# An S4 convolution and mixer block on one core: the inverse transform of the first half moved to the last steps and the pause behind them, three store buffers, other queues for x and w1, w1 and w2 split later

## The chip, the cores and the metric

The kernel runs on one core of a Trainium2 chip. The metric is the device time of one execution in microseconds, as the median of several runs. All data are float32; on TensorE weights of the mixer are held as two float32r parts, a high and a low one.

## What is computed

With h a layer norm of x scaled and shifted by a conditioning vector, a state-space convolution over 2048 positions and 512 channels is added to x, then a token-mixing and a channel-mixing MLP. The reference, cut to what matters:

```python
def _A_ref(u, A_re, A_im, B_re, B_im, C_re, C_im, log_dt, Dskip):
    P = jnp.exp(logdA[:, :, None] * l[None, None, :])
    K = jnp.einsum("dn,dnl,dn->dl", Cc, P, dB).real
    Yf = rfft2(pad(up)) * rfft2(pad(K))
    return irfft2(Yf)[..., :L] + u * Dskip
def _B_ref(x, w1, w2, w3, w4):
    h = _gelu(_layernorm(x) @ w1)
    x1 = x + shifted_channel_groups(h) @ w2
    return x1 + _gelu(_layernorm(x1) @ w3) @ w4
x = A_u
h = _layernorm(x) * (1 + ca) + sa
x = x + ga * _A_ref(h, ...)
h = _layernorm(x) * (1 + cb) + sb
x = x + gb * _B_ref(h, w1, w2, w3, w4)
```

## The kernel before, in words

The order of every engine's instructions is the order in which the code records them; the tile framework adds the semaphore waits. SP, ACT and POOL issue DMAs, each in its own order, so a DMA that waits holds up what its engine issues after it. Stages:

1. *To about 212 us.* The convolution's kernel K is built (exponentials, sines, products on DVE, matmuls); x's first transform is written to DRAM as VU. On the side POOL copies w3, w4 and w2 to DRAM scratch (WD, L506 to L512).
2. *k_first (L619), 212 to 224.* Eight rounds of matmuls turn K (in KX) into the two halves VK[0], VK[1]. T2 and TU are tables; T3 holds negated columns of T2, made by POOL in `flip` (L658).
3. *The sixteen steps (L1096 to L1150), 225 to 304.* A step is (jh, kc): half jh of the channels, block kc of the frequencies. In step n PE does `spectrum_k` (sk, L680, 32 matmuls on T2, T3 and VK), then `back` of step n-1 (L702, with the table Gm), then `spectrum_u` of step n+1 (su, L650, on a VU block). DVE's `multiply` (L690, L692) makes four products and two sums, zc. ACT copies su's banks to us (three copies) and back's banks pz to z (two copies), and z is stored to DRAM as ZT[jh] by two DMAs of 256 KB on POOL. `load_vu` reads the VU block of a later step into a ring of seven blocks (ldp, tile "ld").
4. *Back over positions.* `inverse(jh, g)` (two `inv_half`, L726 to L734) takes four blocks of ZT[jh], reread by `load_inv` (L717), and the table FI, and adds the result to X2, the residual x, which `load_x` puts in the place of KX once k_first has read that. Groups g = 0 and 3 use blocks 0, 3, 4, 7; groups 1 and 2 use 1, 2, 5, 6. For the first half the four groups run in steps 12, 13, 15 and behind the steps, into the pz, pk2 and py banks of PSUM. `half_stat` (L783) takes half statistics of X2 rows.
5. *The hole (L1151 to L1181).* After the last step ZT[1] must be stored and reread before anything else can go on: about 304 to 316. PE runs dummy matmuls there (`keep`).
6. *The mixer.* Token mixing (w1, w2), then channel mixing (w3, w4); TensorE is nearly full there.

w1 and w2 are split by `weights` (L743): a load, then for each of four row blocks a copy to float32r on ACT (high part) and a subtraction on DVE (low part). Before, w1 is staged through the ldp ring and split in steps 9 and 10, w2 in steps 14 and 15. A z tile has two buffers, so the copy of step n waits for the store of step n-2.

Of the kernel before, what the change touches and what calls it, by code (L numbers as in the profile page):

```python
# [106 lines left out]
def body(ctx, tc, A):  # L107
# [439 lines left out]
    with tc.manual_schedule():  # L547
# [49 lines left out]
        for f in later:  # L597
# [6 lines left out]
    v0x = ExitStack()  # L604
    c2 = a2.enter_context(pool("c2"))
    TU = TU[0]
    Gm = c2.tile([128, 2, 64], F32, name="Gm")
    FI = c2.tile([128, 32, 2, 32], F32, name="FI")
    VK = [v0x.enter_context(pool("v0", side="right")).tile([128, 64, 2, 64], F32, name="VK0"),
          c2.tile([128, 64, 2, 64], F32, name="VK1")]  # L610
    ldp = a2.enter_context(pool("ldp", bufs=7))
    s2x = ExitStack()
    s2 = s2x.enter_context(pool("s2", bufs=2))
    psa = s2x.enter_context(pool("psa", bufs=2, space=PSUM))
# [38 lines left out]
            act(us[:, n], q[n % 2])  # L653
        return us

    t3s = {}

    def flip(kc):  # L658
        t = t3s[kc] = c2.tile([128, 8, 64], F32, name="T3", bufs=3)
        for gh in range(2):  # L660
            r = slice(gh * 64, gh * 64 + 64)
            P.tensor_scalar(t[r], T2[kc // 4][r, kc % 4 * 4:kc % 4 * 4 + 8, 64 - gh * 64:128 - gh * 64], -1.0, None, op0=OP.mult)

    def spectrum_k(jh, kc):
        p = [kbank([128, 2, 2, 128]) for gh in range(2)]
        for i in range(2):
            for ro in range(2):
                for ri in range(2):
                    for kk in range(2):
                        for gh in range(2):  # L670
                            k1 = kc * 4 + 2 * kk + i
                            rows = slice(gh * 64, gh * 64 + 64)
                            w = T2[k1 // 16][rows, k1 % 16]
                            if ri == gh:
                                w = w[:, ro * 64:ro * 64 + 64]
                            elif ro == ri:
                                w = w[:, gh * 64:gh * 64 + 64]
                            else:
                                w = t3s[kc // 2 * 2][rows, k1 % 8]
                            T.matmul(p[gh][kk * 64:kk * 64 + 64, i, ro], w,  # L680
                                     VK[jh][rows, ri * 32 + k1].rearrange("p j g -> p (j g)"),
                                     start=(ri == 0), stop=(ri == 1), skip_group_check=True)
        return p
# [10 lines left out]

    def back(jh, kc):
        zc = zcs.pop((jh, kc))
        z = s2.tile([128, 4, 256], F32, name="z")
        o = [psa.tile([128, 2, 256], F32, name="pz") for kk in range(2)]
        for n in range(2):
            for kk in range(2):  # L700
                r = slice(kk * 64, kk * 64 + 64)
                T.matmul(o[kk][n * 64:n * 64 + 64], Gm[r, n], zc[n][r], start=True, stop=True, skip_group_check=True)  # L702

        def store(q, a, b):
            for n in range(2):
                q.dma_start(dram(ZT[jh], n * 16384 + (kc * 4 + a) * 256, [[32768, 32], [8192, 2], [1, (b - a) * 256]]),
                            z[n * 64:n * 64 + 64, a:b].rearrange("p k d -> p (k d)"))

        last = (jh, kc) == (1, 7)
        for kk in range(2):  # L710
            act(z[:, 2 * kk:2 * kk + 2], o[kk])
            if last:
                store((Y, S)[kk], 2 * kk, 2 * kk + 2)
        if not last:
            store(P, 0, 4)

    def load_inv(jh, k, i=None, q=Y):  # L717
        if (jh, k) not in zis:
            zis[jh, k] = block()
        a, n = (0, 4) if i is None else (2 * i, 2)  # L720
        q.dma_start(zis[jh, k][:, a:a + n], dram(ZT[jh], (k * 4 + a) * 32768, [[256, 128], [32768, n], [1, 256]]))

    def load_x(g):
        Y.dma_start(X2[:, g * 4:g * 4 + 4].rearrange("p b d -> p (b d)"), A["x"][g])

    def inv_half(jh, g, i, pl, name):  # L726
        p = pl.tile([128, 2, 256], F32, name=name)
# [8 lines left out]
    def inverse_parts(jh, g, pl, name):  # L736
        return [inv_half(jh, g, i, pl, name) for i in range(2)]
# [5 lines left out]
    def weights(pl, src, rows, cols, name, ntile):  # L743
        hi = pl.tile([128, ntile, cols], F32R, name=name + "h")
        lo = pl.tile([128, ntile, cols], F32R, name=name + "l")

        def load(stage, i, m=1, c0=0, c1=cols):
            n = min(128, rows - i * 128)
            w = stage(m, c1 - c0) if stage else lo.bitcast(F32)[:, i:i + m, c0:c1]
            Y.dma_start(w[:n], src[i * 128:i * 128 + (m - 1) * 128 + n, c0:c1].rearrange("(a p) n -> p a n", p=n))  # L750

            def split():
                for j in range(m):
                    h = hi[:n, i + j, c0:c1]
                    act(h, w[:n, j])
                    V.tensor_sub(lo[:n, i + j, c0:c1], w[:n, j], h.bitcast(F32))  # L756
            return split
        return hi, lo, load

    def two(m, n):  # L760
        return block().rearrange("p (a c) b -> p a (c b)", a=2)

    def rstd(r, v):
        n = r.shape[-1]
# [326 lines left out]

    def split_w(n):
        for _ in range(n):
            splits.pop(0)()

    steps = [(jh, kc) for jh in range(2) for kc in range(8)]  # L1096
    with tc.manual_schedule():
        load_vu(*steps[0])
        flip(0)
        Y.dma_start(Gm, A["G"].rearrange("p (a b) -> p a b", a=2))  # L1100
        for r in range(8):
            k_first(r)
            if r == 3:
                load_vu(*steps[1])
            if r == 6:
                load_vu(*steps[2])
        us = spectrum_u(*steps[0])
        split = None
        for n, st in enumerate(steps):
            p = spectrum_k(*st)  # L1110
            multiply(*st, us, p)
            if n == 7:
                v0x.close()
                pw2 = ctx.enter_context(pool("pw2", side="right", reuse_waits="tile"))
                pw1 = ctx.enter_context(pool("pw1", side="right", reuse_waits="tile"))
                W2h, W2l, ldw2 = weights(pw2, WD["w2"], 512, 512, "w2", 4)
                W1h, W1l, ldw1 = weights(pw1, A["w1"], 512, 512, "w1", 4)
# [12 lines left out]
            if n == 9:  # L1130
                Y.dma_start(FI, A["FI"].rearrange("p (a b c) -> p a b c", a=32, b=2))
            if split:
                split()
                split = None
            if n in (8, 9):
                split = ldw1(two, n % 2 * 2, 2)
            if n == 10:
                for k in (0, 3, 4, 7):
                    load_inv(0, k)
            if n == 12:  # L1140
                inverse(0, 0)
                w2s = [ldw2(None, 2 * i, 2) for i in range(2)]
                for b in range(4):
                    half_stat(b, 0)
            if n == 13:
                inverse(0, 3)
                for k in (1, 2, 5, 6):
                    load_inv(0, k)
            if n in (14, 15):
                w2s.pop()()  # L1150
        for f in i1:  # L1151
            f()
        back(*steps[15])
        s2x.close()
        tp = lambda name, bufs=1, **k: pool(name, bufs, reuse_waits="tile", **k)
        cm = ctx.enter_context(tp("cm", 2, side="right"))
        hv = ctx.enter_context(tp("hv", side="right"))
        gop = ctx.enter_context(tp("gop", 2, side="right"))
        psT = ctx.enter_context(tp("psT", space=PSUM))
        psw = ctx.enter_context(tp("psw", 2, space=PSUM))  # L1160
        psy = a2.enter_context(tp("psy", 2, space=PSUM, side="right"))
# [4 lines left out]

        for k, i in ((3, 1), (0, 0)):
            load_inv(1, k, i, Y)
            load_inv(1, k + 4, i, S)
        for k, i in ((3, 0), (0, 1)):  # L1170
            load_inv(1, k, i)
            load_inv(1, k + 4, i)
        for i in range(2):
            inv_half(0, 2, i, psy, "py")()
        for b in (14, 15, 4, 5, 6, 7):
            half_stat(b, 0)
        for k in (1, 2):
            load_inv(1, k)
            load_inv(1, k + 4)
# [122 lines left out]
```

## Time and profile before

| | |
|---|---|
| runs, us | 688.12, 691.77, 688.82 (median 688.82) |
| profiled execution, us | 691.26 |
| its span, first to last instruction, us | 689.5 |
| mean granted TensorE clock | 0.989 |
| busy in the span: PE, DVE, ACT, POOL, us | 642.6, 498.0, 331.2, 124.8 |
| DMA over the span | 86.42 MB, mean 125 GB/s |

The span is the profiled execution's; 1.8 us lie around it. Times in the text are us from the start of the span. An instruction row gives start, length, engine, line, operation, out<-in with the shapes, a count, and in brackets the idle time before it with what ended it. A line may be that of a helper (L115 is every ACT copy), so the tile names tell what an instruction is: pz<-zc is back, pk<-ld su, pk<-VK sk, ZT<-z a store, ld<-VU and ld<-ZT the reads.

### The profile page before, as it was taken

The page shows a single profiled execution, that of the slowest core. Times are in us where ns is not written, and L with a number is a line of the kernel's source. Part 1 is how long each engine was busy: PE and PEld are TensorE (multiplying, and loading weights), DVE is VectorE, ACT ScalarE, POOL GpSimd, SP SyncE. Part 2 cuts the span into 40 slices and gives each one's busy share as a digit, 9 for nine tenths or more (in the row PEclk, how much of TensorE's full clock was granted, in tenths as well). Part 3 has the DMA queues.
Part 4 walks back from the last instruction along what each step waited for, and adds up shares of the span by engine and source line. Part 5 has one row for each costly group of instructions (what it writes and reads, how often), then busy time and mean ns, then how long its engine had stood idle before and what let it go on. Part 6 is the DMA issues. An engine that isn't in the chain of part 4 may idle for free.

```text
span 689.5 us, 16884 instructions
## 1 busy us (share of the span) xinstructions
PE 642.6 (93%) x7195; PEld 509.2 (74%) x7195; DVE 498.0 (72%) x795; ACT 331.2 (48%) x505; POOL 124.8 (18%) x236
## 2 busy tenths in 40 slices
PE   1899999999999998977998999999999999999996
PEld 0456655655569776634887889999899889898895
DVE  7899999999996887986987967464574536363522
ACT  3878988889875557432444623123131312222121
POOL 4011112112103355413741101001010000000000
PEclk9999999999999999998999999999999999999999
DMA  8603264643739997967387010020100201010001
GB/s 299 284 2 79 75 218 105 209 121 85 275 85 317 354 335 258 346 204 226 108 257 240 1 32 32 16 77 15 47 31 17 77 1 62 1 49 13 1 31 31
DMA packets 51091, 86.42 MB, mean 125 GB/s; under 512 B 4676, under 2 KB 39496, under 8 KB 48424
## 3 DMA queue, kind: packets, MB, share of 16 engines
q1 hardware_dynamic: 46712, 66.74, 30.1%
q0 software_dynamic: 3440, 17.57, 7.4%
q8 instruction: 56, 0.92, 0.6%
q10 hardware_dynamic: 864, 1.05, 0.5%
q14 instruction: 19, 0.16, 0.1%
HBM read 59.12 MB, written 32.90 MB: 133 GB/s over the span
## 4 chain that ended last, share of the span: by engine, by line
PE 70%; DVE 6%; DMA 5%; ACT 3%; POOL 2%; issue 1%; ACTq 0%; SPq 0%; DVEq 0%; POOLq 0%
PE pm L841 7%; PE pm L838 7%; PE pm L839 7%; PE xx L448 7%; PE pa L954 6%; PE pa L955 6%; PE pa L962 6%; PE kp L498 3%; DMA ZT<-z 3%; PE ph L893 2%; PE ph L895 2%; PE ph L892 2%; DMA ld<-ZT 2%; PE pu L426 2%; PE pT L803 2%; PE pk L626 2%
## 5 line engine op out<-in xcount | busy, mean ns | idle before, releaser
L115 ACT ACTIVATE gh<-pm 128x512 fp32r<-128x512 f32 (+1 forms) x48 | 26.9, 560 | 200.7 <-PE pm L841 200.7
L838 PE MATMUL pm<-nh,w3h 128*128 128x256 f32 (+1 forms) x352 | 86.6, 281 | 2.7 <-ACT nh L115 2.7
L839 PE MATMUL pm<-nh,w3l 128*128 128x256 f32 (+1 forms) x352 | 86.3, 280 | 0.1
L946 DVE TENSOR_TENSOR gl<-gf,gh 128x512 fp32r<-128x512 f32 (+1 forms) x48 | 30.8, 643 | 68.4 <-ACT gf L115 68.4
L954 PE MATMUL pa<-w4h,gh 128*128 128x512 f32 (+1 forms) x176 | 69.6, 395 | 0.0
L838 PEld LDWEIGHTS pm<-nh,w3h 128*128 128x128 f32 (+1 forms) x352 | 66.0, 187 | 4.4 <-ACT nh L115 2.9
L955 PE MATMUL pa<-w4l,gh 128*128 128x512 f32 (+1 forms) x176 | 68.9, 392 | 0.0
L839 PEld LDWEIGHTS pm<-nh,w3l 128*128 128x128 f32 (+1 forms) x352 | 65.9, 187 | 2.2 <-DVE w3l L756 0.5
L765 POOL TENSOR_TENSOR rs<-mv,eps_t 128x1 f32<-128x1 f32 (+1 forms) x39 | 11.0, 282 | 282.4 <-DVE mv L771 265.4
L841 PE MATMUL pm<-nl,w3h 128*128 128x256 f32 (+1 forms) x352 | 55.0, 278 | 0.0
L449 PE MATMUL xx<-MG,ON 64*128 64x512 f32 x160 | 48.1, 397 | 0.0
L962 PE MATMUL pa<-w4h,gl 128*128 128x512 f32 (+1 forms) x176 | 48.0, 390 | 0.0
L448 PE MATMUL xx<-MG,ON 64*128 64x512 f32 x160 | 48.0, 396 | 0.0
L841 PEld LDWEIGHTS pm<-nl,w3h 128*128 128x128 f32 (+1 forms) x352 | 47.0, 187 | 0.0
L898 DVE TENSOR_TENSOR h<-h,ph 128x512 f32<-128x512 f32 x16 | 11.0, 687 | 45.1 <-PE ph L895 45.1
L466 DVE SCALAR_TENSOR_TENSOR e<-tr,p 128x512 f32<-128x512 f32 x64 | 41.1, 684 | 1.5 <-ACT tr L115 1.5
L498 PEld LDWEIGHTS kp<-e,e 128*32 128x32 f32 x2048 | 30.1, 110 | 12.7 <-issue 7.6
L475 DVE TENSOR_TENSOR e<-tr,p 128x1024 f32<-128x1024 f32 x32 | 39.0, 1220 | 0.0
L476 DVE TENSOR_TENSOR e<-tr,m 128x1024 f32<-128x1024 f32 x32 | 39.0, 1219 | 0.0
L115 ACT ACTIVATE p<-xx 128x1024 f32<-128x1024 f32 (+1 forms) x40 | 37.5, 979 | 2.2 <-PE xx L252 1.0
L962 PEld LDWEIGHTS pa<-w4h,gl 128*128 128x128 f32 (+1 forms) x176 | 33.0, 188 | 7.3 <-DVE gl L946 0.2
L115 ACT ACTIVATE tr<-xx 128x1024 f32<-128x1024 f32 x32 | 33.0, 1030 | 9.6 <-PE xx L449 7.9
(236 smaller groups left out, 1731.6 us busy)
## 6 DMA issues: line engine op xcount, KB each, us to landing
VU<-vs SPq DMA_DIRECT2D x64, 128.0 KB, 3.7
ld<-VU SPq DMA_DIRECT2D x16, 512.0 KB, 7.4
ZT<-z POOLq DMA_DIRECT2D x30, 256.0 KB, 6.2
ld<-ZT SPq DMA_DIRECT2D x12, 512.0 KB
Dw<-in_w POOLq DMA_DIRECT2D x8, 688.0 KB, 4.7
xu<-in_u SPq DMA_DIRECT2D x4, 1024.0 KB, 8.0
KX<-in_x SPq DMA_DIRECT2D x4, 1024.0 KB, 8.0
GD<-go SPq DMA_DIRECT2D x16, 256.0 KB, 2.3
```

Of the source, the lines that this page charges most:

```text
L115: return S.activation(out, in_, f, bias=bias, scale=scale)
L448: T.matmul(x[:, :512], la, ma, start=(i == 0), stop=(i == len(ops) - 1))
L449: T.matmul(x[:, 512:], lb, mb, start=(i == 0), stop=(i == len(ops) - 1))
L466: V.scalar_tensor_tensor(e0[:, 1, a], tr[:, 1, 0], 1.0 - 2.0 * a, mg[:, a], op0=OP.mult, op1=OP.mult)
L475: V.tensor_mul(e0[:, 0], tr[:, 0, 0:1].to_broadcast([128, 2, 512]), mg)
L498: T.matmul(kp[32 * j:32 * j + 32, (k % 2) * 4 + g], e1[:, r, d], e0[:, r, :, d * 32:d * 32 + 32], start=(r == 0), stop=(r == 1), skip_grou ...
L838: T.matmul(p, wh[:, k, c], hi[k], start=(k == 0), stop=False)
L839: T.matmul(p, wl[:, k, c], hi[k], start=False, stop=False)
L841: T.matmul(p, wh[:, k, c], lo[k], start=False, stop=(k == 3))
L954: T.matmul(acc[i], gh[:m, e, s], W4h[:m, f], start=(f == 0), stop=False)
L955: T.matmul(acc[i], gh[:m, e, s], W4l[:m, f], start=False, stop=False)
L962: T.matmul(acc[i], gl[:m, e, s], W4h[:m, f], start=False, stop=(f == 10))
```

## The change

- z gets three buffers. T3 becomes one tile for all 32 frequencies, filled by eight POOL instructions before the steps; before, two instructions every second step filled one of three small tiles.
- The ldp ring has six blocks, not seven. Blocks 0, 3, 4, 7 of ZT[0] get four own buffers (zi), where VK[0] lay, and are read in step 9. w2's tiles, which lay there, come behind the steps.
- inverse(0, 0) moves from step 12 to step 14, inverse(0, 3) from 13 to 15, in the pz banks; group 1 moves behind back(15), its adds into the hole.
- x blocks and w1 are loaded by POOL's queue, w1 from a DRAM copy. FI is loaded before the steps. Gm takes FK's place, so its load follows k_first. A VU block is asked for four steps ahead, not three.
- w1: the high parts are copied in steps 13 and 14, the low parts made in the hole. w2 is loaded by POOL after the last steps and split wholly in the hole. Two rereads of ZT[1] go from ACT's queue to POOL's.

The diff, without its unchanged surroundings:

```diff
-    WD = {k: dpool.tile(list(A[k].shape), F32, name="D" + k) for k in ("w2", "w3", "w4")}
+    WD = {k: dpool.tile(list(A[k].shape), F32, name="D" + k) for k in ("w1", "w2", "w3", "w4")}
...
-        side[28 + 3 * k].append(lambda i=k * 256: P.dma_start(WD["w2"][i:i + 256], A["w2"][i:i + 256]))
+        for j, w in enumerate(("w1", "w2")):
+            side[24 + 4 * j + 2 * k].append(lambda w=w, i=k * 256: P.dma_start(WD[w][i:i + 256], A[w][i:i + 256]))
...
-    ldp = a2.enter_context(pool("ldp", bufs=7))
+    ldp = a2.enter_context(pool("ldp", bufs=6))
...
+    T3 = s2.tile([128, 32, 64], F32, name="T3", bufs=1)
+
+    def flip(i):
+        for a in range(0, 16, 8):
+            for gh in range(2):
+                r = slice(gh * 64, gh * 64 + 64)
+                P.tensor_scalar(T3[r, i * 16 + a:i * 16 + a + 8], T2[i][r, a:a + 8, 64 - gh * 64:128 - gh * 64], -1.0, None, op0=OP.mult)
...
-        z = s2.tile([128, 4, 256], F32, name="z")
+        z = s2.tile([128, 4, 256], F32, name="z", bufs=3)
...
-            zis[jh, k] = block()
+            zis[jh, k] = block() if jh or k in (1, 2, 5, 6) else zip_.tile([128, 4, 256], F32, name="zi")
...
-        Y.dma_start(X2[:, g * 4:g * 4 + 4].rearrange("p b d -> p (b d)"), A["x"][g])
+        P.dma_start(X2[:, g * 4:g * 4 + 4].rearrange("p b d -> p (b d)"), A["x"][g])
...
             if n > 0:
                 back(*steps[n - 1])
-            if n == 15:
-                i1 = inverse_parts(0, 1, psb, "pk2")
             if n < 15:
                 us = spectrum_u(*steps[n + 1])
-            if n + 3 < 16:
-                load_vu(*steps[n + 3])
-            if n % 2 == 0 and n < 14:
-                flip(steps[n + 2][1])
-            if n in (3, 4, 6, 8):
-                load_x(n - 3 if n < 5 else n // 2 - 1)
+            if n + 4 < 16:
+                load_vu(*steps[n + 4])
+            if n in (2, 4, 6, 8):
+                load_x((0, 3, 1, 2)[n // 2 - 1])
+            if n in (9, 10):
+                w1s.append(ldw1(None, n % 9 * 2, 2, q=P))
+            if n in (13, 14):
+                w1s[n - 13] = w1s[n - 13]()
             if n == 9:
-                Y.dma_start(FI, A["FI"].rearrange("p (a b c) -> p a b c", a=32, b=2))
...
-            if n == 10:
                 for k in (0, 3, 4, 7):
                     load_inv(0, k)
             if n == 12:
+                for k in (1, 2, 5, 6):
+                    load_inv(0, k)
+            if n == 14:
                 inverse(0, 0)
-                w2s = [ldw2(None, 2 * i, 2) for i in range(2)]
                 for b in range(4):
                     half_stat(b, 0)
-            if n == 13:
+            if n == 15:
                 inverse(0, 3)
...
         back(*steps[15])
+        i1 = inverse_parts(0, 1, psb, "pk2")
...
+        w2s = ldw2(None, 0, 4, q=P)
...
-            load_inv(1, k + 4, i, S)
+            load_inv(1, k + 4, i, P)
...
+        w2s = w2s()
+        for f in i1:
+            f()
         for i in range(2):
             inv_half(0, 2, i, psy, "py")()
         for b in (14, 15, 4, 5, 6, 7):
             half_stat(b, 0)
+        for f in w1s:
+            f()
+        w2s()
```

What this does to three queues. SP in the second part of the steps, before (ld<-VU a VU block, KX<-in_x an x block, ld<-in_w w1, ld<-ZT the rereads):

```order
L724 DMA KX<-in_x 128x2048
L750 DMA ld<-in_w 128x2x512
L640 DMA ld<-VU 128x4x256
L1131 DMA FI<-in_FI 128x2048
L750 DMA ld<-in_w 128x2x512
L640 DMA ld<-VU 128x4x256
L721 DMA ld<-ZT_61 128x4x256 x4
L640 DMA ld<-VU 128x4x256 x2
L750 DMA w2l<-Dw_64 128x2x512 x2
L721 DMA ld<-ZT_61 128x4x256 x4
```

and SP from its first VU block to the same place, after (FK<-in_G is Gm, zi the own buffers):

```order
L640 DMA ld<-VU 128x4x256 x4
L1106 DMA FI<-in_FI 128x2048
L1108 DMA FK<-in_G 128x128
L640 DMA ld<-VU 128x4x256 x10
L721 DMA zi<-ZT_61 128x4x256 x4
L640 DMA ld<-VU 128x4x256 x2
L721 DMA ld<-ZT_61 128x4x256 x4
```

Ten VU blocks now follow Gm without a break, and the last two, 14 and 15, stand behind the four rereads into zi, as they stood behind four rereads before.

POOL in the steps, before (T is T3, made by flip; ZT<-z a store's halves):

```order
L662 TENSOR_SCALAR T_3081<-xu 64x512 x2
L662 TENSOR_SCALAR T_3355<-xu 64x512 x2
L706 DMA ZT_61<-z 32x2x1024 x4
L662 TENSOR_SCALAR T_3500<-xu 64x512 x2
L706 DMA ZT_61<-z 32x2x1024 x4
```

and after, to the end of the steps and the hole:

```order
L706 DMA ZT_61<-z 32x2x1024 x4
L724 DMA KX<-in_x 128x2048
L706 DMA ZT_62<-z 32x2x1024 x2
L750 DMA w1l<-Dw_64 128x2x512
L706 DMA ZT_62<-z 32x2x1024 x2
L750 DMA w1l<-Dw_64 128x2x512
L706 DMA ZT_62<-z 32x2x1024 x10
L750 DMA w2l<-Dw_65 128x4x512
L721 DMA ld<-ZT_62 128x2x256 x2
```

The flips between the stores are gone; x, w1 and w2 stand there in their place, and two rereads of ZT[1] follow w2.

DVE from the last step's sums to the first add of the second half, before (zc the sums, KX the adds and their statistics):

```order
L692 TENSOR_TENSOR zc_4495<-mb 128x2x2x128
L756 TENSOR_TENSOR w2l<-w2l,w2h 128x512 x2
L734 TENSOR_TENSOR KX<-pk_4515,KX 128x2x256
L734 TENSOR_TENSOR KX<-pk_4524,KX 128x2x256
L734 TENSOR_TENSOR KX<-py,KX 128x2x256 x2
L784 BN_STATS st_80<-KX 128x6 x6
L734 TENSOR_TENSOR KX<-py,KX 128x2x256
```

and after:

```order
L692 TENSOR_TENSOR zc_4449<-mb 128x2x2x128
L734 TENSOR_TENSOR KX<-pz,KX 128x2x256 x2
L734 TENSOR_TENSOR KX<-pk_4502,KX 128x2x256
L734 TENSOR_TENSOR KX<-pk_4511,KX 128x2x256
L734 TENSOR_TENSOR KX<-py,KX 128x2x256 x2
L784 BN_STATS st_81<-KX 128x6 x6
L758 TENSOR_TENSOR w1l<-w1l,w1h 128x512 x4
L758 TENSOR_TENSOR w2l<-w2l,w2h 128x512 x4
L734 TENSOR_TENSOR KX<-py,KX 128x2x256
```

The adds of inverse(0, 3), from pz, now follow the last sums, and eight subtractions for w1 and w2 stand ahead of the last row, the add that ends the hole.

More of the change, by code (lines that the diff above doesn't have):

```diff
@@ L606, in body @@
     TU = TU[0]
-    Gm = c2.tile([128, 2, 64], F32, name="Gm")
     FI = c2.tile([128, 32, 2, 32], F32, name="FI")
@@ L654, in spectrum_u @@
         return us
[L656 to L662, printed above, removed]
+    T3 = s2.tile([128, 32, 64], F32, name="T3", bufs=1)
[4 more added lines that the diff above has]
+                P.tensor_scalar(T3[r, i * 16 + a:i * 16 + a + 8], T2[i][r, a:a + 8, 64 - gh * 64:128 - gh * 64], -1.0, None, op0=OP.mult)
     def spectrum_k(jh, kc):
@@ L678, in spectrum_k @@
                             else:
-                                w = t3s[kc // 2 * 2][rows, k1 % 8]
+                                w = T3[rows, k1]
                             T.matmul(p[gh][kk * 64:kk * 64 + 64, i, ro], w,
@@ L745, in weights, with load, low @@
         lo = pl.tile([128, ntile, cols], F32R, name=name + "l")
-        def load(stage, i, m=1, c0=0, c1=cols):
+        def load(stage, i, m=1, c0=0, c1=cols, q=Y):
             n = min(128, rows - i * 128)
             w = stage(m, c1 - c0) if stage else lo.bitcast(F32)[:, i:i + m, c0:c1]
-            Y.dma_start(w[:n], src[i * 128:i * 128 + (m - 1) * 128 + n, c0:c1].rearrange("(a p) n -> p a n", p=n))
+            q.dma_start(w[:n], src[i * 128:i * 128 + (m - 1) * 128 + n, c0:c1].rearrange("(a p) n -> p a n", p=n))
             def split():
                 for j in range(m):
-                    h = hi[:n, i + j, c0:c1]
-                    act(h, w[:n, j])
-                    V.tensor_sub(lo[:n, i + j, c0:c1], w[:n, j], h.bitcast(F32))
+                    act(hi[:n, i + j, c0:c1], w[:n, j])
+                def low():
+                    for j in range(m):
+                        V.tensor_sub(lo[:n, i + j, c0:c1], w[:n, j], hi[:n, i + j, c0:c1].bitcast(F32))
+                return low
             return split
         return hi, lo, load
-    def two(m, n):
-        return block().rearrange("p (a c) b -> p a (c b)", a=2)
     def rstd(r, v):
@@ L1093, in split_w @@
         for _ in range(n):
-            splits.pop(0)()
+            splits.pop(0)()()
     steps = [(jh, kc) for jh in range(2) for kc in range(8)]
@@ L1099, in body @@
         flip(0)
-        Y.dma_start(Gm, A["G"].rearrange("p (a b) -> p a b", a=2))
+        flip(1)
         for r in range(8):
             k_first(r)
-            if r == 3:
-                load_vu(*steps[1])
+            if r in (1, 3, 5):
+                load_vu(*steps[r // 2 + 1])
             if r == 6:
-                load_vu(*steps[2])
+                Y.dma_start(FI, A["FI"].rearrange("p (a b c) -> p a b c", a=32, b=2))
+        Gm = pa12.tile([128, 2, 64], F32, name="FK")
+        Y.dma_start(Gm, A["G"].rearrange("p (a b) -> p a b", a=2))
         us = spectrum_u(*steps[0])
-        split = None
+        w1s = []
         for n, st in enumerate(steps):
@@ L1113, in body @@
                 v0x.close()
[L1114 removed]
                 pw1 = ctx.enter_context(pool("pw1", side="right", reuse_waits="tile"))
[L1116 to L1117 removed]
+                W1h, W1l, ldw1 = weights(pw1, WD["w1"], 512, 512, "w1", 4)
+                zix = ExitStack()
+                zip_ = zix.enter_context(pool("zi", bufs=4, side="right", reuse_waits="tile"))
             if n > 0:
                 back(*steps[n - 1])
[L1120 to L1121 removed]
             if n < 15:
                 us = spectrum_u(*steps[n + 1])
[L1124 to L1137 removed]
+            if n + 4 < 16:
[6 more added lines that the diff above has]
+                w1s[n - 13] = w1s[n - 13]()
+            if n == 9:
                 for k in (0, 3, 4, 7):
@@ L1140, in body @@
             if n == 12:
+                for k in (1, 2, 5, 6):
+                    load_inv(0, k)
+            if n == 14:
                 inverse(0, 0)
-                w2s = [ldw2(None, 2 * i, 2) for i in range(2)]
                 for b in range(4):
                     half_stat(b, 0)
-            if n == 13:
+            if n == 15:
                 inverse(0, 3)
[L1147 to L1152, printed above, removed]
         back(*steps[15])
+        i1 = inverse_parts(0, 1, psb, "pk2")
         s2x.close()
+        zix.close()
         tp = lambda name, bufs=1, **k: pool(name, bufs, reuse_waits="tile", **k)
@@ L1158, in body @@
         gop = ctx.enter_context(tp("gop", 2, side="right"))
+        pw2 = ctx.enter_context(tp("pw2", side="right"))
+        W2h, W2l, ldw2 = weights(pw2, WD["w2"], 512, 512, "w2", 4)
+        w2s = ldw2(None, 0, 4, q=P)
         psT = ctx.enter_context(tp("psT", space=PSUM))
```

## The prediction

> **What bounds the kernel now.** I read the stage windows first, then the waits in the stage that the change touches, then the chain through the pause before the second half, then the timelines. The windows from 186 us on (columns: stretch, its length, busy us of PE, PEld, DVE, ACT and POOL, granted clock, share of the DMA engines, GB/s):
>
> ```profile
> 186.00:201.00 15.00, 15.00 (x284) 9.46 (x278) 14.68 (x18) 12.74 (x19) 0.00 (x0) 1.00 0.19 42
> ...
> 224.40:264.00 39.60, 36.87 (x796) 28.36 (x798) 31.04 (x51) 21.95 (x43) 16.93 (x20) 1.00 0.99 348
> 264.00:284.00 20.00, 17.11 (x370) 13.49 (x366) 18.99 (x31) 13.01 (x26) 10.93 (x12) 1.00 0.82 262
> 284.00:304.00 20.00, 18.46 (x368) 10.84 (x360) 19.27 (x35) 10.61 (x22) 7.30 (x10) 1.00 0.85 289
> 304.00:316.00 12.00, 5.22 (x47) 2.82 (x47) 3.70 (x9) 0.34 (x1) 0.00 (x0) 0.85 0.76 231
> ```
>
> The sixteen steps fill 225 to 304, the pause ("the hole") 304 to 316. In the steps three things are nearly full at once: PE, DVE and, to 264, the DMA engines at 0.99. Who waits there, from the waits of 224 to 318 (us in total, times, longest):
>
> ```profile
> ACT z L115 <- DMA ZT<-z: 8.7, 3, 4.3
> PE py L731 <- DMA ld<-ZT: 6.5, 1, 6.5
> PE pk L680 <- POOL T L662: 1.6, 3, 0.5
> ```
>
> The copies into z wait for a store to leave one of two buffers, PE waits a little for the flips, and in the hole PE waits for the reread of ZT. The pace is read from the first matmul of back() in PE's timeline, steps 0, 5, 6 and 11, and from DVE's first product of two steps in a row:
>
> ```profile
> 230.45 0.65 PE L702 MATMUL pz<-zc,Gm 64*64 64x512 f32 x2 [0.48 <-DVE zc L692]
> ...
> 252.59 0.59 PE L702 MATMUL pz<-zc,Gm 64*64 64x512 f32 x1
> 256.45 0.61 PE L702 MATMUL pz<-zc,Gm 64*64 64x512 f32 x1
> 281.39 0.65 PE L702 MATMUL pz<-zc,Gm 64*64 64x512 f32 x2 [1.02 <-DVE zc L692]
> ```
> ```profile
> 253.22 0.69 DVE L690 TENSOR_TENSOR ma<-pk,us 128x512 f32<-128x512 f32 x1 [0.23 <-PE pk L680]
> 256.82 0.69 DVE L690 TENSOR_TENSOR ma<-pk,us 128x512 f32<-128x512 f32 x1
> ```
>
> A step in which nothing is late takes PE 3.86 us and DVE 3.60. From back() of step 0 to that of step 11 it took 50.94, where 11 x 3.86 = 42.5: 8.5 us of stalls. The chain through the hole, in order of time (start, us, what):
>
> ```profile
> 301.59 1.64 PE pz L702 x8
> ...
> 305.03 2.69 DMA ZT<-z
> ...
> 313.63 2.42 PE py L731 x17
> 316.07 0.70 DVE KX L734
> ```
>
> From back(15) at 301.59 to the first add of the second half at 316.07 is 14.5 us, nearly all of it DMA.
>
> **The change part by part.** The measuring point is that add; what follows it keeps its order.
>
> *Ahead of the steps, nothing.* Two more 512 KB copies, w1's, stand among the w4 and w2 copies on POOL; they can finish in the 186 to 201 row, where DMA is at 0.19. Without that room they would cost up to 3 us. The flips become eight at the front, POOL's earlier four being
>
> ```profile
> 209.31 6.20 POOL L662 TENSOR_SCALAR T<-xu 64x512 f32<-64x512 f32 x4 [26.16 <-DMA wm<-in_TU]
> ```
>
> or 12.4 us, done by 221.7. The chain there runs through k_first (L626), su of step 0 (L650) and sk of step 0 (L680), the first reader of T3:
>
> ```profile
> 223.54 0.89 PE pk L626 x16
> 224.43 1.02 PE pk L650 x16
> 225.45 1.82 PE pk L680 x64
> ```
>
> so the flips have 3.7 us of cover, and would cost PE what they exceed it by. Gm's load now waits on SP for the last matmul of k_first, at 224.4, and VU blocks 4 to 15 queue behind it: DMA work starts again at about 226. Gm is wanted at 230.45.
>
> *Three z buffers, flips and w1's splits gone from the steps.* This removes the cause of the 8.5 us. If nothing else were late, back() of step 12 would start at 230.45 + 12 x 3.86 = 276.8, and VU block 14, read just ahead of the next step, would be wanted at 277.7.
>
> *What is late next: the DMA engines.* Sizes from the DMA view (KB each, us to landing):
>
> ```profile
> ld<-VU SPq DMA_DIRECT2D x16, 512.0 KB, 7.4
> ZT<-z POOLq DMA_DIRECT2D x30, 256.0 KB, 6.2
> ld<-ZT SPq DMA_DIRECT2D x12, 512.0 KB
> KX<-in_x SPq DMA_DIRECT2D x4, 1024.0 KB, 8.0
> w2l<-Dw SPq DMA_DIRECT2D x2, 512.0 KB, 9.0
> ```
>
> Before VU block 14 lands these have to go through: VU 4 to 14, 11 x 0.524 = 5.8 MB; the four x blocks, 4.2; stores of steps 0 to 9, 5.2; w1, 1.05; and the four ZT blocks that SP now issues ahead of VU 14, 2.1: together 18.3 MB. At 348 GB/s, the stretch that kept the queues full, that is 52.6 us from 226, so 278.6; at 312, the mean of the three step rows weighted by length (348 x 39.6 + 262 x 20 + 289 x 20, over 79.6), 58.7, so 284.7. I take 284, near the late end, because SP issues VU 14 only behind ZT reads that wait for step 7's store, and a VU block so issued in a crowd is slow, as these two were:
>
> ```profile
> L640 SPq DMA_DIRECT2D ld<-VU x2: 359/409/459, 278.3 to 278.7; - x2
> ...
> DMA to landing us min/median/max: 7.4/7.4/7.4
> ```
>
> From its landing L the rest is a chain: su and us 2.6 (PE 1.0, ACT 1.6, rows above and below), multiply(14) 3.6, the two adds of inverse (0,0) 1.3, four half statistics 1.4, multiply(15) 3.6, the two adds of (0,3) 1.3, which now stand before back(15) because both use the pz banks: with hand-overs L + 14. PE's work on the inverses lies beside the products.
>
> ```profile
> 255.17 1.59 ACT L115 ACTIVATE us<-pk 128x512 f32<-128x512 f32 x3
> ...
> 285.36 1.28 DVE L734 TENSOR_TENSOR KX<-pz,KX 128x512 f32<-128x512 f32 x2
> 286.55 1.40 DVE L784 BATCH_NORM_STATS2 st<-KX 128x6 f32<-128x256 f32 x4
> ```
>
> So back(15) starts at 284 + 14 = 298, against 301.59: 3.6 us gained. Off that I take 1.0 (0 to 4) for step 13's copy into z, which the inverse (0,0) needs out of the pz banks: its buffer is freed by step 10's store, among the same reads.
>
> *The x blocks and w1 on POOL's queue.* They stand between stores there. The price is that a store lands later. Three buffers cover 3 x 3.86 = 11.6 us between copy and reuse; stores landed in at most 8.9 us before:
>
> ```profile
> DMA to landing us min/median/max: 2.9/6.2/8.9
> ```
>
> At nothing, then, with 2.7 us of cover; without it up to 2 us per x block. The Trainium skill's "DMA: Bandwidth & Descriptors", in "Queues, rings and completion order", says that each DMA engine takes turns between queues a packet at a time and consumes one queue's ring in order. By that rule stores that follow x in one ring come about 3 us later (an estimate: 1.05 MB at this trace's 348 GB/s), so the cover would just fail, and the sum would be up to 1 us worse; the 8.9 us above, with x in the other queue, shows that taking turns did not keep stores quick.
>
> *The hole.* DVE's work there becomes: adds of i1 and of (0,2), 2.6; six half statistics 2.1; eight low parts of w1 and w2, of the adds' shape and taken at their 0.6, 4.8. That is 9.5 of the 14.5 us, so it hides, if w2 has come. w2's load (1.05 MB, 3.0 us of DMA at 348) goes beside step 15's store and ahead of the rereads; DMA there has 24% of 12 us, 2.9, free. Between 0 and 3.0 I take 1.2. Behind the hole, with six blocks in the ring instead of seven, two rereads instead of one wait for the first blocks to be read: 0 to 1.5, taken at 0.
>
> Sum: -3.6 + 1.0 + 1.2 = -1.4 us. The profiled execution took 691.26 (span 689.5), 2.4 above the median of 688.82; put on the median, 687.4. About 0.5%, 3.4 us, is what a measurement of this kernel can tell from no change.
>
> **The rivals.**
>
> *A, the DMA engines keep up.* VU 14 is there by 277.7. Then PE and DVE set the end: back(13) at 280.6, su 1.0, inverse (0,0) about 2 (17 of its matmuls took 2.42 in the chain above), adds 1.3, statistics 1.4, multiply 3.6, adds 1.3: back(15) at 291.2, 10.4 earlier, less 1.2: 679.6. For it: 348 GB/s is a rate with many 1 KB rows, and FI and w2 have left the stage. Against: PE, DMA and DVE would all have to run without a gap. The Trainium skill's same page, "Specifications", gives 358 GB/s as one core's HBM limit, which would put L at 277.1 and so this rival in force; the 348 of this trace is 3% under it. In between A and the forecast lies an L of 278 to 282, 2 to 6 us faster than forecast.
>
> *B, VU 14 is the new wait.* Should the engines share evenly among all that is outstanding, VU 14 lands with the last: step 7's store lands at about 268 (back(7) at 257.5, copy and issue 2, up to 8.9), and then 2.1 of ZT, 1.05 of VU, 1.05 of x, 1.05 of w1 and 1.6 of stores, 6.8 MB, take 20 to 22 us: L = 290, back(15) at 305, with the hole +4.6: 693.4. It costs time from L = 285.4 on, and over 3.4 us from L = 288.8. For it: the 7.4 us of the two VU blocks, where a block's own data is 1.5 us at 348 GB/s. Against: SP's earlier blocks, with fewer others about, came faster.
>
> *C, w2 comes late into the hole.* Its low parts stand on DVE ahead of the add that ends the hole. They need ACT's four copies (2.0) and 2.4 us of DVE before it; so w2 must land by about 10 us after back(15) starts. Issued 1.6 after it, with the 9.0 us that such loads took, it is there at 10.6. Each us more costs one; at 3 us, 690.4.
>
> *D, the buffers do not do it.* If stores behind x take over 11.6 us, the wait for z stays at four places, 1 to 2 us each; but then DMA is the bound anyway and L hardly moves: no difference, 688.8.
>
> **How the numbers follow.** Forecast with C and D as its edge (within 0.5%): 0.43. A and the space between: 0.36, of which A in full 0.12. B, alone or with C: 0.21. The forecast 687.4 is the likeliest case's. Low end 681.0, short of A in full; high end 693.5, B. Faster by over 0.5% (under 685.4) 0.36, within 0.43, slower (over 692.3) 0.21.
>
> **What would show it.** In the profile after: waits of z for ZT stores gone or small up to step 8; no wait for the flips; back(12) near 277; then one wait of PE for ld<-VU of 4 to 9 us, the step that decides; the DMA share near 1 from 226 to 290; in the hole DVE's last low part done before the py matmul. No PE wait for VU means A; one that ends after 288, B; the add waiting for w2l, C. A gain or loss that arises before 225 or after the first add would make the whole account wrong.

## The result, and the profile after

The changed kernel takes 694.78 us (693.76 to 695.38, 5 runs) against 688.87 (688.12 to 691.77, 5 runs): a ratio of 1.0075, 95% interval [1.0052, 1.0098]. It is slower by 5.9 us; the forecast was 687.4, in a range of 681.0 to 693.5. Its profiled execution took 695.38 with a span of 693.6, against 691.26 and 689.5.

The stage windows of after, the stretches shown of before (length, busy us of PE, PEld, DVE, ACT, POOL, granted clock, DMA share, GB/s):

```profile
224.40:264.00 39.60, 37.13 (x879) 30.87 (x875) 34.38 (x57) 24.42 (x48) 10.99 (x20) 1.00 0.93 325
264.00:284.00 20.00, 14.45 (x340) 11.67 (x332) 16.68 (x28) 10.59 (x21) 6.88 (x12) 0.98 0.99 347
284.00:304.00 20.00, 15.80 (x268) 10.03 (x272) 10.98 (x20) 8.17 (x16) 2.77 (x5) 0.85 0.67 203
304.00:316.00 12.00, 4.36 (x58) 2.25 (x46) 9.54 (x18) 2.39 (x5) 1.60 (x3) 0.77 0.71 219
```

The DMA engines are now full to 284 instead of 264, PE and DVE lose time from 264 on, and TensorE's clock is down from 284 on, which before it was not until the hole. The waits of 224 to 318 (us in total, times, longest):

```profile
POOL ld L721 <- DMA ZT<-z: 7.4, 1, 7.4
...
PE pk L650 <- DMA ld<-VU: 6.3, 1, 6.3
ACT w2h L115 <- DMA w2l<-Dw: 5.8, 1, 5.8
```

The copies into z wait for no store any more, and no row names the flips. PE waits once for a VU block, 6.3 us. SP's own queue shows why that block comes late (waits of 240 to 300):

```profile
SPq L721 <- DMA ZT<-z: 14.2, 1, 14.2
```

SP stands 14.2 us at the first read into zi, until a store of ZT[0] has landed. It issues the four reads from 266.0 on, and VU 14, which stands behind them, at 272.2. PE's timeline of after at back() of steps 0 and 12, at the matmul that waits, at back(15) and at the reread that ends the hole:

```profile
229.36 1.25 PE L702 MATMUL pz<-zc,FK 64*64 64x512 f32 x6 [0.48 <-DVE zc L692]
...
278.45 0.63 PE L702 MATMUL pz<-zc,FK 64*64 64x512 f32 x2
...
285.98 1.13 PE L650 MATMUL pk<-ld,wm 64*64 64x256 f32 x8 [6.30 <-DMA ld<-VU]
...
301.35 1.25 PE L702 MATMUL pz<-zc,FK 64*64 64x512 f32 x5 [1.52 <-DVE KX L734]
...
319.29 3.21 PE L731 MATMUL py<-ld,FI 128*32 128x256 f32 x28 [10.93 <-DMA ld<-ZT]
```

(Gm lies in FK's place and bears its name.) back(12) starts 9.0 us earlier than before (287.43). By back(15) all of that is gone, 301.35 against 301.59. Then the hole, from back(15) to the first add of the second half, takes 19.93 us instead of 14.48:

```profile
321.28 0.69 DVE L734 TENSOR_TENSOR KX<-py,KX 128x512 f32<-128x512 f32 x1 [6.90 <-PE py L731]
```

Before, that add was at 316.07. So the add is 5.2 us late, about the whole loss. (The two profiled executions lie 4.1 us apart, since that of the kernel before is one of its slower ones.) The chain of waits of after through it (start, us, what):

```profile
272.19 13.66 DMA ld<-VU
...
285.98 1.99 PE pk L650 x16
287.97 2.91 PE pk L680 x64
...
304.88 5.95 DMA ZT<-z
...
312.27 6.88 DMA ld<-ZT
```

Step 15's store takes 5.95 us where before it took 2.69, and the reread behind it 6.88 instead of 4.98. What ran beside the store is in the two-us windows of after (DMA share and GB/s are the last columns):

```profile
306.00:308.00 2.00, 2.00 (x22) 1.25 (x14) 1.59 (x4) 0.00 (x0) 0.00 (x0) 1.00 0.89 304
308.00:310.00 2.00, 0.36 (x2) 0.00 (x0) 2.00 (x6) 0.00 (x0) 0.00 (x0) 1.00 1.01 395
```

The store is 0.5 MB; these four us moved 1.4 MB, since w2's megabyte, issued 0.4 to 1.5 us before the store's quarters, goes through with it. The quarters go out on SP's and ACT's queues and w2 on POOL's, so w2 does not stand ahead of them in a queue; what they share is the DMA engines.

### The profile page after: what moved, and what is told of

It is laid out like the page before. It is cut to its first block, busy times and chain, and to the rows that moved or that the text cites. A ratio compares the mean times of both kernels' runs of the same rounds, so it can differ in the third digit from the quotient of the medians.

```text
span 693.6 us, 16875 instructions
## 1 busy us (share of the span) xinstructions
PE 635.7 (92%) x7195; PEld 507.8 (73%) x7195; DVE 497.0 (72%) x795; ACT 331.3 (48%) x505; POOL 118.8 (17%) x239
## 4 chain that ended last, share of the span: by engine, by line
PE 62%; DVE 26%; DMA 5%; issue 4%; ACT 2%; POOL 1%; SPq 0%; ACTq 0%; DVEq 0%; POOLq 0%
PE pm L841 7%; PE pm L839 7%; PE pm L838 7%; PE pa L962 6%; PE pa L954 6%; PE pa L955 6%; DVE e L466 4%; DVE e L476 4%; DVE e L475 4%; PE pk L680 4%; DVE m L472 2%; PE ph L893 2%; PE ph L892 2%; PE ph L895 2%; DMA ld<-VU 2%
## 5 line engine op out<-in xcount | busy, mean ns | idle before, releaser
L449 PE MATMUL xx<-MG,ON 64*128 64x512 f32 x160 | 47.1, 390 | 0.0
L448 PE MATMUL xx<-MG,ON 64*128 64x512 f32 x160 | 47.1, 390 | 0.0
L680 PEld LDWEIGHTS pk<-VK,xu 64*64 64x64 f32 x768 | 34.7, 137 | 5.0 <-issue 3.7
```

Source lines behind the costliest of these rows:

```text
L448: T.matmul(x[:, :512], la, ma, start=(i == 0), stop=(i == len(ops) - 1))
L680: T.matmul(p[gh][kk * 64:kk * 64 + 64, i, ro], w, VK[jh][rows, ri * 32 + k1].rearrange("p j g -> p (j g)"), start=(ri == 0), stop=(ri == 1 ...
```

## The experiments

Theory 1: VU block 14 is late because SP issues it behind the zi reads, and w2's load slows the last store. Theory 2: the two rereads that went to POOL's queue make the hole long. Theory 3: the bytes of the steps set their end in any order. Theories 4 to 7 are stated where they come up, in what was expected of a run. Each ratio is to the kernel before, timed beside it on the same chip; its median was 688.87 to 689.71 us in these comparisons, so times of different experiments compare to about 0.8 us.

**w2 out of the hole.** Loaded in step 14 through two ring blocks; the split stays.

```diff
+            if n == 14:
+                w2b = [block().rearrange("p (a c) b -> p a (c b)", a=2) for _ in range(2)]
+                for i in range(2):
+                    Y.dma_start(w2b[i], WD["w2"][i * 256:i * 256 + 256].rearrange("(a p) n -> p a n", p=128))
...
-        w2s = ldw2(None, 0, 4, q=P)
```

> The changed kernel, but w2 is loaded in step 14 by SP's queue, through two blocks of the ld ring, and only its split stays in the hole. Theory 1 (w2's 1 MB, issued 0.4 to 1.5 us ahead of the last store, is what makes the hole long): the last store lands in about 2.7 us instead of 6.0, the rereads about 1.5 us sooner than their 6.9, the first add of the second half comes 4.5 us earlier, at about 316.8; 690.3 us against 694.78 (689.3 to 691.5). Theory 2 (the two rereads that moved from ACT's to POOL's queue make the hole long): the store may land sooner, but the add is still late; a gain of at most 2 us, 692.8 or more.

692.83 us, ratio 1.0044 [1.0023, 1.0065]. The store takes 2.73 us again and the hole 15.63, so the mechanism of theory 1 holds. The total fell by 2, not 4.5, and by time alone is not told apart from the change, since the intervals overlap: in the profiled execution, one of the slowest of seven (694.67; they go from 690.19 to 694.74), VU 14 landed 2.3 us later than in after, which took back much of it.

**The rereads back on ACT's queue.**

```diff
-            load_inv(1, k + 4, i, P)
+            load_inv(1, k + 4, i, S)
```

> The changed kernel with the two rereads of ZT[1] back on ACT's queue, nothing else. Theory 1: they are issued about 0.5 us earlier and share the DMA engines with the same others; 0.5 to 1 us gained, 694.0 us. Theory 2: the reread lands in about 5 us instead of 6.9, as before the change, and the add comes 2 to 3 us earlier: 692.3 us or less.

693.36 us, 1.0061 [1.0043, 1.0079]. Between the two forecasts in time, with an interval that overlaps the change's as well; the chain of this run shows the store as slow as in after and the reread as quick as before:

```profile
305.48 6.05 DMA ZT<-z
312.39 4.81 DMA ld<-ZT
317.33 1.97 PE py L731 x16
```

The hole is 17.38. Theory 2 is right too: both causes are there, each for a part.

**VU blocks 14 and 15 ahead of the zi reads.**

```diff
-            if n == 9:
+            if n == 11:
                 for k in (0, 3, 4, 7):
                     load_inv(0, k)
```

> The changed kernel with the four zi reads recorded in step 11, behind the loads of VU blocks 14 and 15, instead of step 9; the same bytes in another order. Theory 1 (the order on SP's queue makes VU 14 late): VU 14 is issued near 256 and lands before it is wanted, PE's wait of 6.3 us for it goes, and what is late next is inverse (0,0) waiting for the zi blocks at about 286; back(15) starts near 295 instead of 301.35; 688.5 us (687 to 690.5). Theory 3 (the DMA engines' bytes are the bound, whatever the order): the wait only passes from su to inverse (0,0) and later stores, back(15) not before 299; 692.5 us or more.

687.86 us, 0.9978 [0.9963, 0.9994]: 6.9 us less than the change. The source view of the VU loads tells when they were issued (first and last of blocks 13 to 15), of after and then of this run:

```profile
L640 SPq DMA_DIRECT2D ld<-VU x3: 360/2493/4642, 251.1 to 276.9; - x3
```
```profile
L640 SPq DMA_DIRECT2D ld<-VU x3: 359/360/360, 250.9 to 259.3; - x3
```

Issued by 259 instead of 272 and 277, they cost PE nothing; back(15) starts at 293.96. The inverse (0,0) did not wait for the zi blocks either. With the same bytes the DMA engines moved more, 376 GB/s from 264 to 284 instead of 347. Theory 3 falls. The 376 is also more than the 358 that the prediction cites as a limit.

**All three edits together.**

> The three edits together: VU 14 and 15 ahead of the zi reads, w2 loaded in step 14, the two rereads on ACT's queue. Theory 1: the gains add, 4.5 and 0.7 in the hole and 6.3 in the steps, 683.3 us (682 to 685.5), under the kernel before. Theory 3: w2's 1 MB now stands among the last reads of the steps and delays them by its 3 us, and the steps gain at most 2: 689 us or more.

682.79 us, 0.9904 [0.9889, 0.9920]. The gains add; the hole is 13.92. Its chain:

```profile
297.75 2.73 DMA ZT<-z
...
306.70 1.97 PE py L731 x16
308.69 0.70 DVE KX L734
```

Between the store and PE's matmuls the profile names no reread here but work of DVE, six half statistics and low parts of w1 and w2: the splits that the change moved into the hole now stand about as late as the rereads.

**w2 back in the hole, the other two edits kept.** This kernel has the diffs of the second and third experiment only.

> The kernel with all three edits, but w2's load back in the hole on POOL's queue: VU 14 and 15 first and the rereads on ACT's queue. Theory 1 alone (w2's megabyte is the loss): the last store takes 6 us instead of 2.7, 687.0 us or more, as slow as with the VU edit alone (687.86). Theory 2 alone (the queue of the rereads is the loss): 683.5 us. Both, 3.2 us for w2 and 2 us for the queue: 685.9 us (685.0 to 686.8).

686.64 us, 0.9953 [0.9933, 0.9972]. The time fits both causes and does not rule out the 687.0 of theory 1 alone. The hole does: at 17.33 it lies between the 13.92 of all three edits and the 19.81 of the VU edit alone, so each cause has its part.

**The kernel before with its two ACT rereads on POOL's queue.**

```diff
-            load_inv(1, k + 4, i, S)
+            load_inv(1, k + 4, i, P)
```

> The kernel before, with one line changed: the two rereads of ZT[1] that ACT's queue issues go to POOL's queue. Theory 2 (a reread from POOL's queue lands later by itself): the rereads land 2 to 2.6 us later and so does the first add of the second half, 691.6 us against 689.38. Theory 1 alone (they landed late because w2 was in the way): no difference, 689.4 us, within 0.6.

690.94 us, 1.0015 [0.9999, 1.0031]: not told apart from no change by time. In the chain the reread takes 5.91 instead of 4.98, and from the store's landing to its start 1.7 us pass instead of 0.8. The hole is 15.84 instead of 14.48; two more runs below that leave it as it was have 14.02 and 14.04. Theory 2's sign, at some half of the size forecast.

The hole of eight kernels, from back(15) to the add, us:

| | rereads on ACT | rereads on POOL |
|---|---|---|
| w2 loaded in the hole | 17.38, 17.33 | 19.93 (the change), 19.81 |
| w2 loaded earlier | 14.48 (before), 13.92 | 15.63, 15.84 |

Pairs that differ in nothing else that bears on the hole put w2's load at 3.4 us (13.92 to 17.33) and 4.3 (15.63 to 19.93), and the queue at 1.4 (14.48 to 15.84), 2.5 (17.33 to 19.81) and 2.6 (17.38 to 19.93); the two larger ones have w2 ahead of the rereads in POOL's queue.

**z with two buffers again**, in the kernel with all three edits.

```diff
-        z = s2.tile([128, 4, 256], F32, name="z", bufs=3)
+        z = s2.tile([128, 4, 256], F32, name="z", bufs=2)
```

> The kernel with all three edits (682.79 us) with z back to two buffers. Theory 6 (the third buffer is what took the z waits out of the steps): waits of z for stores return at three or four steps, 1 to 4 us each, back(12) comes 4 to 7 us later than its 280.1, 688 us (686 to 690). Theory 3 (the DMA engines' bytes set the pace, so a z wait only takes the place of another): within 1 us of 682.8.

686.77 us, 0.9951 [0.9933, 0.9969]. The waits of ACT for stores are back:

```profile
ACT z L115 <- DMA ZT<-z: 15.7, 7, 3.7
```

Yet back(12) starts 51.1 us behind back(0), just as with three buffers. The 4 us arise behind it: back(12) to back(15) takes 17.2 instead of 14.7, and the hole 15.3 instead of 13.9. In the code the inverses there need the pz banks that z is copied from; that this is the cause is not shown by a run. Neither theory foresaw that place.

**The kernel before with three z buffers**, the ring cut to six blocks to make room.

```diff
-        z = s2.tile([128, 4, 256], F32, name="z")
+        z = s2.tile([128, 4, 256], F32, name="z", bufs=3)
...
-    ldp = a2.enter_context(pool("ldp", bufs=7))
+    ldp = a2.enter_context(pool("ldp", bufs=6))
```

> The kernel before with three buffers for z, and the ld ring cut from seven blocks to six to make room; nothing else. Theory 6 (the z waits are the cause of the 8.5 us of stalls to step 11): back(12) starts 50 us behind back(0) instead of 57, and the time falls by 2 to 4 us, to 686 to 688. Theory 7 (the bytes of the stage are the cause, and the z wait is only where they show): back(12) stays within 1.5 us of 57 behind back(0), 689.7 us within 1.

691.29 us, 1.0026 [1.0009, 1.0044]. No z wait is left, and back(12) starts 54.5 us behind back(0) instead of 57.0, where the whole change gained 7.9. Another execution of the unchanged steps, in the run with the rereads on POOL's queue, has 55.6, so the gain is 1.0 to 2.5 us. It lies ahead of back(8): from back(0) to back(8) it took 33.4 us (36.0 before, 34.7 in that other run), from back(8) to back(12) 21.1 (21.0 before). Further on PE waits 5.6 us for a reread of ZT[0], before back(15) (probably the ring's missing block), and the kernel is slightly slower.

**The kernel before with FI loaded ahead of the steps.** The load moves from step 9 to the place behind k_first's load of VU 2.

```diff
             if r == 6:
                 load_vu(*steps[2])
+                Y.dma_start(FI, A["FI"].rearrange("p (a b c) -> p a b c", a=32, b=2))
...
-            if n == 9:
-                Y.dma_start(FI, A["FI"].rearrange("p (a b c) -> p a b c", a=32, b=2))
```

> The kernel before with FI's load (1.05 MB) moved from step 9 to k_first, ahead of the steps; the z buffers stay two. Theory 7: the steps have 3 us of DMA less in front of back(12), which starts 54 us behind back(0) instead of 57; 687 us (686 to 688.5), if the reads of ZT behind it don't take it back. Theory 6: the z waits stay and so does the time, 689.7 us.

688.22 us, 0.9990 [0.9978, 1.0001]; back(12) 55.7 behind back(0). The two executions of the unchanged steps have 57.0 and 55.6, so this tells nothing apart: theory 7 is not borne out.

**Dummy matmuls while PE waits for VU 14**, in the changed kernel. Their results are overwritten.

```diff
+            if n == 13:
+                d = [psa.tile([128, 2, 256], F32, name="pk1") for _ in range(2)]
+                for a in range(28):
...
+                                T.matmul(d[gh][kk * 64:kk * 64 + 64, 0, c * 128:c * 128 + 128], T2[0][r, a % 16, :64],
+                                         VK[1][r, a].rearrange("p j g -> p (j g)"),
```

> The changed kernel with 224 dummy matmuls of the size of spectrum_k's (about 6.3 us of PE) put ahead of spectrum_u of step 14, where PE waited 6.3 us for VU block 14; their results are overwritten. Theory 4 (the idle PE loses its clock, granted 0.50 from 284 to 290, and su and sk behind the wait then take 4.9 us instead of 2.8): they run at full clock, back(15) comes about 2 us earlier, 692.7 us against 694.78 (691.8 to 693.4). Theory 5 (they are slow because the DMA engines are full, whatever PE did before): no change, 694.8 us.

704.69 us, 1.0214 [1.0183, 1.0245]. The dummies were mis-sized: each is two matmuls in the profile, and they kept PE busy to 298. Behind them the clock is full and su's start to ma takes 3.2 us instead of 4.9. PE also stalled among them, with no wait that the profile names:

```profile
284.03 3.82 PE L1129 MATMUL pk<-VK,xu 64*64 64x128 f32 x128 [1.84 <-issue]
290.22 7.99 PE L1129 MATMUL pk<-VK,xu 64*64 64x128 f32 x213 [2.37 <-issue]
```

**The same with 96 dummies** (12 in place of 28 in the loop above).

> The changed kernel with 96 dummy matmuls ahead of spectrum_u of step 14 (the run with 224 kept PE busy 19 us instead of the 6.3 meant, since each counts as two in the profile; 96 are about 5.5 us and a stall). Theory 4 (the idle PE loses its clock): from su's start to the product ma behind it 3.2 us, as in that run, instead of 4.9; 693.1 us against 694.78 (692.2 to 694.0). Theory 5 (full DMA engines slow them): 4.9 us still, 694.8 us.

697.03 us, 1.0115 [1.0095, 1.0135], against both forecasts. The granted clock stays at 1.00 throughout, as theory 4 says, but sk behind su now stalls, and su's start to ma takes 5.2 us:

```profile
291.46 0.55 PE L680 MATMUL pk<-VK,xu 64*64 64x128 f32 x11 [1.80 <-issue]
```

Also su starts at 287.6, behind the last dummies, 1.7 us later than in after. So the remedy cost more than the slow clock; no run shows the clock's part alone in the whole time.

**More dummies in the hole** of the kernel with all three edits.

```diff
-        keep(6)
+        keep(20)
```

> The kernel with all three edits (682.79 us), with 20 instead of 6 dummy matmuls of keep in the hole, so that PE is idle there for about 1 us instead of 4.9. Theory 4: the 16 matmuls of py before the first add run at full clock, 1.0 us instead of 2.0, and the add comes 1 us earlier; 681.6 us (681.0 to 682.2). If the rereads come earlier than the last dummy, or the low parts of w2 are what PE waits for: 682.8 us.

681.75 us, 0.9896 [0.9875, 0.9917], the fastest here and 7.6 us under the kernel before. By time alone it is not told apart from the 682.79; the hole tells, with 12.96 instead of 13.92 us. The row of the matmul ahead of the add, with all three edits and then with the dummies as well:

```profile
306.70 3.64 PE L731 MATMUL py<-ld,FI 128*32 128x256 f32 x32 [4.91 <-DVE w2l L1183]
```
```profile
305.74 1.93 PE L731 MATMUL py<-ld,FI 128*32 128x256 f32 x32 [1.48 <-DMA ld<-ZT]
```

The 32 matmuls take 1.93 us instead of 3.64. The window 304 to 308 of this run has the clock at 1.00; with six dummies the same window has 0.51. What ends the hole is now DVE, whose add follows the last low part of w2 without a pause:

```profile
304.57 2.49 DVE L1183 TENSOR_TENSOR w2l<-ld,w2h 128x512 fp32r<-128x512 f32 x4
306.99 0.68 DVE L734 TENSOR_TENSOR KX<-py,KX 128x512 f32<-128x512 f32 x1
```

By this trace a shorter wait for DMA alone would gain nothing more at the add; the splits would have to leave the hole too.

## Why the prediction was wrong

**The step that failed** is the hole's: "Between 0 and 3.0 I take 1.2." It measured 5.45, for two reasons. The first is the argument "DMA there has 24% of 12 us, 2.9, free": that share is a mean over the hole, while the hole is a chain, and a load issued just ahead of the store lengthens that link, so that every link behind it starts later. Even the upper bound, w2's own 3.0 us, was short of the 3.3 that the store alone lost. The second is a term that was missing: the move of two rereads to POOL's queue stood among the changes, and the sum gave it no price. The table puts it at 1.4 to 2.6. Rival C looked at w2 from the wrong side: the last low part ended at 314.4, well ahead of the add at 321.28; it was w2's reading that cost, not its use. Only with both costs gone, in the last run above, do the low parts set the add.

**The steps came out 2.4 us worse** than the forecast back(15) of 299.0 (298 and 1.0 for the z copy). VU 14 landed at 285.85 against L = 284, and PE's one wait of 6.3 us lies in the forecast 4 to 9: mechanism right, size 1.9 short. The 7.4 us taken for a block in a crowd became 13.7, behind four reads in the same queue. From L to back(15) it took 15.5 us instead of 14, where the slow clock stands: "su and us 2.6" became 4.9. Of that 1.7 is the clock's, as the last section shows, since behind the 224 dummies it took 3.2. The other 0.6 is a term left out: the products waited not for ACT's copies but for PE's sk of step 14, which comes between. The 1.0 us for step 13's z copy did not arise.

**Right:** nothing before the steps; no flip or z wait; back(12) at 278.45 for 276.8; POOL's stores behind x landing in at most 8.1 us, and no 3 us later (median 6.0, before 6.2); that VU 14 is the step that decides; and that nothing of size comes after the add (1.1 us came back there). Rival B did not decide: with L at 285.85, back(15) came where it was before. The run with VU 14 and 15 ahead of the zi reads shows that their place in SP's order, and not the bytes, made them late. By the bytes the sum had 18.3 MB through by 278.6 to 284.7, and no cheaper order was priced.

**Right with the wrong cause:** "This removes the cause of the 8.5 us" put the gain down to z, the flips and w1's splits together. Up to step 12 the third buffer was worth 1.0 to 2.5 us in the run that had it alone, with one ring block less. From back(8) to back(12) the change took 16.3 us instead of 21.0, where three buffers alone left 21.1; there the kernel before was short of DVE, not of buffers. Its window and one of its low parts of w1:

```profile
264.00:288.00 24.00, 21.11 (x470) 16.36 (x466) 22.99 (x40) 14.62 (x29) 14.34 (x16) 1.00 0.86 286
```
```profile
271.48 1.29 DVE L756 TENSOR_TENSOR w1l<-ld,w1h 128x512 fp32r<-128x512 f32 x2 [1.01 <-ACT w1h L115]
```

DVE was busy for 23 of 24 us; four low parts (3.0 us) and the adds and statistics of the inverse (0,0) (2.7) left this stretch. That fits the 4.7 us, but no run took them out singly. Up to back(8) the change gained the other 3.2 us (32.8 instead of 36.0). The third buffer can be most of it, with its 33.4, but two executions of the same steps differ by 1.3 there and no run took out the flips singly, so the shares stay open.

## What to carry to other kernels

Where a stage ends in a chain of store and reread, price what is issued ahead of each link, and on which queue, not the mean share of the DMA engines. A load that the next step wants must be issued ahead of bulk reads that are wanted later; here that order alone was worth 6.9 us. And every line of a diff needs a price, one that only names another queue too. Work moved into a pause hides only as long as the pause lasts: the splits, free in the change's 19.9 us, set the end of the last kernel's 13.0.

## What the runs showed of the hardware

*TensorE's clock halves when PE waits, and stays so for some us.* Windows of after:

```profile
280.00:282.00 2.00, 0.00 (x0) 0.00 (x0) 2.00 (x5) 0.80 (x2) 0.91 (x2) 1.00 1.06 400
282.00:284.00 2.00, 0.00 (x0) 0.00 (x0) 0.60 (x1) 0.00 (x0) 0.16 (x1) 0.81 1.08 362
284.00:286.00 2.00, 0.02 (x3) 0.05 (x4) 0.00 (x0) 0.00 (x0) 0.00 (x0) 0.50 1.09 369
...
288.00:290.00 2.00, 2.00 (x44) 2.00 (x40) 0.00 (x0) 1.95 (x4) 0.00 (x0) 0.50 1.12 354
290.00:292.00 2.00, 2.00 (x48) 1.35 (x44) 1.09 (x2) 0.91 (x3) 0.00 (x0) 0.98 0.94 301
```

PE went idle at 279.7, the clock fell to half some 3.5 us later, and came back about 4 us after work resumed at 285.98. In between su took 1.99 us instead of 0.86 and sk 2.91 instead of 1.9. The Trainium skill's "TensorE: Matmul & The Clock Gate", in "Part 1: The HAM clock gate (the "warmup" mystery)", has the clock at half after an idle window of about 3.4 us and full after a busy one of as much; the trace agrees. The run with 224 dummies shows that a shorter stop can do it as well: PE stood from 287.9 to 290.2 (and for 1.8 us up to 284.0), and the clock is at 0.59 and 0.56 in the two windows from 290 to 294. In after, the wait of 6.3 us cost some 2 us more than itself.

*PE's instructions seem to wait for full DMA engines.* The page of after:

```profile
PE 635.7 (92%) x7195; PEld 507.8 (73%) x7195; DVE 497.0 (72%) x795; ACT 331.3 (48%) x505; POOL 118.8 (17%) x239
...
q8 instruction: 56, 0.92, 0.6%
```

56 packets of 0.92 MB are 16.4 KB each; over PE's 14,390 instructions that is 64 bytes for one, and a packet holds 256 of them, 128 matmuls with their weight loads. With 192 matmuls more, in the run with 96 dummies, that queue has 58 packets, and with 448 more 60, as that count asks. The unnamed stalls of the dummies lay 128 matmuls apart, and came only while the DMA share was above 1. The Trainium skill's "Runtime: NRT & Kernel Launch", in "Instruction fetch mechanics", tells of refills in blocks of 16 KiB whose cost is mostly hidden; if the stalls are such refills, here it was not. In the kernel with all three edits such stalls are the longest wait of PE in the steps:

```profile
PE pk L680 <- issue: 4.8, 5, 1.6
```

Against it stands the kernel before: its DMA share is above 1 in 18 of the 33 two-us windows from 224 to 290, yet its PE has no such wait in the steps. So full engines are not enough, and what else it takes is open. No run took this cause away by itself; it is argued, not shown.
